# Batch 2's first dense layer by seven half-size products, with a new written order

## The chip, the cores and the metric

The kernel runs on one core of a Trainium2 chip. The metric is the device time of one execution in microseconds, the median of several runs. The engines are TensorE (PE; its weight loads are listed as PEld), VectorE (DVE), ScalarE (ACT), GpSimd (POOL) and SyncE (SP). PE multiplies into PSUM; DVE and ACT read PSUM; POOL does not touch it here. Every engine works through its own queue strictly in the order in which the instructions were written, and semaphores make it wait for the others. POOL and SP also issue the DMAs.

## The reference

Attention over four batches (8 heads, 768 positions, head size 64) in which a position sees the first 4 positions and the last 128, and then two dense layers with a squared ReLU between them:

```python
keep = (pos[None, :] < 4) | ((rel >= 0) & (rel < 128))
a = softmax(where(keep, q @ k.T / 8, -1e9))      # per batch and head
x = (a @ v), heads side by side                  # 3072 x 512
h = x @ w_in                                     # 512 x 2048
g = maximum(h, 0) ** 2
out = g @ w_out                                  # 2048 x 512, float32 out
```

## The kernel before

Products are in bf16 with float32 sums. The work goes batch by batch: loads, transposes of queries and keys (on PE for batches 0 and 1, by DMA transposes from SP for batches 2 and 3), scores, exps on ACT, masks on DVE or POOL, values, normalization on DVE, the transposed tokens `xT`, the first dense layer, ReLU and square, the second dense layer, evacuation, store. A batch has 768 tokens, handled as three slices of 256 (s = 0, 1, 2); attention's scores are made in pairs of head pairs for each slice.

**The first dense layer, plain** (`layer1`, L741). `w_in` lies in `w_in_sb` as 4 column groups by 4 row blocks. A group of output blocks is multiplied into one PSUM tile `pm` (L752), a ReLU goes from `pm` to `r` on ACT or DVE (L763, L765), and a square from `r` to `gT_sb` (L772, L774). For batches 1 and 2 there are eight groups of 512 tokens (slices 0 and 1) and four of 256 (slice 2).

**The first dense layer by seven products** (`layer1_fast`, L799, and `quad`, L845), in the kernel before for batch 3 alone. The token matrix, the weights and the output are each cut in two by two blocks. Seven products of sums and differences of blocks give the four output blocks for which eight would be needed otherwise (Winograd's or Strassen's scheme). The sums of weight blocks are `wi_sb[1, 2, 5, 6, 7]` (`weight_sums_in`, L781), made once on DVE; products 3 and 4 use `w_in_sb` itself. The sums of token blocks are made for slice 0 alone (halves of 128 columns, after a `spread` copy) and for slices 1 and 2 together (halves of 256 columns). Then `quad` runs twice for slice 0 and four times for slices 1 and 2. One `quad` works in the two PSUM banks of one tile `y`:

- product 1 into bank 0, product 2 into bank 1;
- `first` copies bank 0 to the SBUF tile `t`, and `less` subtracts bank 1 from `t`;
- product 5 overwrites bank 0, and `less` subtracts it from `t`;
- product 4 adds into bank 1, product 3 into bank 0;
- a ReLU of both banks goes to `r1`, and its square to `gT_sb`;
- product 6 adds into bank 0, product 7 into bank 1, `final` (a DVE instruction that adds `t` and clips at zero) goes to `r2`, and its square to `gT_sb`.

Each product there is 8 matmuls of 128 columns (slice 0) or 4 of 256.

**The second dense layer** (`layer2_fast`, L1006) is made by seven products in all batches but for the first two slices of batch 0. It needs four sums of blocks of `gT_sb` on DVE (L1029), and its results are put together on DVE and ACT (L1080 to L1143) in `osb`, which SP stores (L1148).

**Rooms.** PSUM has four tiles of two banks (`att` 2, `den` 2), which scores, values, transposes and both layers share. In SBUF the pool `qr` has five rooms: they hold loaded queries and keys (`qn`, two for a batch), one weight sum of the second layer for a while, and in the kernel before two of the five weight sums of the first layer; the other three lie in `qkT_all[0]`, where batch 2's transposed queries and keys were.

**The order.** Every piece of work is an `Op` in a plan. `ORDER` (L21 to L53) is a list of all ops by number, written out: the ops are emitted in that order, each on the engine that its letter names (d for DVE, a for ACT, g for POOL, otherwise its first choice), and so each engine's queue is fixed. Keys, planned durations, margins and groups in the code do not influence the program; they served the search that wrote the list. `after`, `takes` and `reads` bind the order and the rooms.

Of the kernel before, what the change touches and what calls it, by code (L numbers as in the profile page):

```python
# [13 lines left out]
BF16 = mybir.dt.bfloat16  # L14
# [6 lines left out]
ORDER = """  # L21
0 8 7 9 1 5 10 11 2 12 13 3 14 15 55d 57+0 16 19 59a 20 17 56d 21 18 61d 63+0 22 58 62d 65a 60d 64 6 67a 83+1 79 66a
68d 69+1 85 70 71d 103+0 84+0 105 73g 74d 72d 23 75+1 86 76 77d 91+0 78a 24 87+1 93 25 89 88 92+0 80 26 114+1 90 94
95+0 4 96 117 97 106g 99+1 98 104+0 107 100d 101 118g 81+1 102d 113+0 108d 156 115 127 82 116d 119+1 157a 121 27 28
120 109+0 111 29 30 31 32 33 158a 122 162 110 112 123+1 125 168 126a 124d 163d 171 169d 164d 165 172a 173d 159 166a
167a 128 131 130d 129d 177 160a 133a 132a 137 145 140 174 148 161d 178d 179d 136 144 289 290 146 149d 170d 147d 138
139d 134 141d 135 175d 34 208g 291 35 36 37 38 39 40 41 42 43 44 45 46 47 48 49 50 51 52 53 54 355 356 292 150 142
143 151 293 294 274 295 152 154 153d 296 297a 176a 298a 155d 186 275 187a 276 277 196+0 180 198a 183 181a 182a 184a
197 204+1 205 199d 188d 200+0 201 192+0 193 189 206a 207d 194d 203d 195d 190d 202a 219+0+0 191d 185d 357 358 359 220
222 278 279 212+0+1 213 215 300 209 301 280 281 373 385d 223 302 237+0+0 210+1 282 299 374 375 376 211 238 240 304  # L30
305 214 239d 306d 230+0+0 307 308 233 231 216 303 311 309d 310 217+0 221 224+0 312 315 234g 232g 313 218 360 314 225
235+0 283 316 241d 242+0 236 317a 284 243 361 362 363 364 365 366 367 368 369 370 371 226+1 228 251+0 229d 286a 227a
244+0 246 252d 253d 245a 285 247d 389 287d 248+1 390 392 340 249d 250d 256+0+0 341a 325 259 257 391 260d 393 326d
386 254+0 322 258g 382 255 342a 263+0+0 323a 261+1 334 262 324d 335d 264 266 265g 396 383 379 288 378 372 267d 331
397 399 398 327a 337 268+0 332d 377 380 384 381 269 319 338a 339d 270+0 271a 272 320d 400 273a 336a 333a 328 321d
329d 330d 456 394 401 352 343 437 353a 349 344a 402 395 530 560g 531 532 533 551 534 535 536 537 538 539 458 318 405
350a 457 351d 441 443d 439 438 345d 406 408 346 412 442 444 445 415 553 403 347d 413 447 409g 416g 428 348a 446a 549
554 548 407g 429 440 448 449 450 414d 451 460 387 354a 461 452 431 388 410 417 475 476 453 454a 479 411 432g 430g
480 463 481a 459 477 418 478 421 482 483 550 552 455 419 422 484a 424 555 404 465a 423g 425g 420 462a 485 433 486
487 490 464 434 488 426 672 489 466 427 467 468 471 580 540 541 542 543 544 545 491 492d 469 494 581 583 470 472  # L40
473d 503 670 495d 435 493 556 559 436 558 557 496a 564 500 565 567 504d 669 509 501d 566 587 510a 512 505a 588 590
568 561 673 511d 497 513d 571 515 574 671 498d 499a 569 572 506 502d 570 514d 516a 575 573 603 521 606 604 507d 522d
546 584g 591g 605g 547 527 576 562 577 518 517a 508a 528a 612 613 582d 631 632 633 519a 563 520a 589g 524 596 597
598g 578 474 579 529a 599 616 617 618a 614 525d 615 585 619 607g 635 592 620 623 586 523a 637a 674a 526d 621d 600d
636 601 625 593 594 622 675 608 638 609 641 602 634 678 624 627 610 626 628 629d 679+1 639 693+1 642 695d 650 651
681a 630 595 640a 680 682 683 694 697 611 654 643 646 656a 676 655 644 645 652 696 677 684 653 709 698 710 647 699
657 660 659a 658 661 708 700 648a 701d 685 686 707 662 665 703 702a 687a 663 664 666 688d 704 705 667a 689 739+0
741a 690 668 649 740 753+0 725+1 754 691 755a 711+1 757 743 706a 727a 726 712 742 756 758 744 692a 713a 745 746 729
714 759 715 760 747a 748a 749 750 767 728 730 716 761a 751 752d 731 732 733a 717 718 763 719a 735 736 764 721 722
769 762d 768 737 720a 738a 765 770 771 773a 772 774 775 778 723 766a 776a 734a 777 724d 779 782 780 786 787 790 791  # L50
792a 781 788 789 805 783 784a 793 794 797 795d 796 806 809 810 798 799 785 807 800 808 812 811d 815 801 802 803d 804
814d 813 816 818 819 824 817 820 821 822 823
"""  # L53
# [58 lines left out]
def kernel(  # L112
# [11 lines left out]
    nc = tc.nc  # L124
# [256 lines left out]
    def load_natural(b, s, older_values):  # L381

        begun = [ops["layer1", b - 2, 0, 0], w_out_op[3]]
        for ti in (1, 0):
            if s == 0:
                qn_slot[b, ti] = Slot("qr", NT)
            for i in range(2):
                t = 2 * s + i

                def run(e, t=t, ti=ti):  # L390
                    if t == 0:
                        qn_t[b, ti] = bank(qn_slot[b, ti], "qn", [128, NT, DM], BF16)
                    return [nc.gpsimd.dma_start(
                        out=qn_t[b, ti][:, t, :].rearrange("p (h d) -> p h d", d=D),
                        in_=(q, k)[ti][b, :, 128 * t:128 * t + 128, :].rearrange("h p d -> p h d"))]
                o = dma_op("pool", ("qk", b, ti, t), run, 64 * 0.032,
                           None,
                           [qn_slot[b, ti]] if t == 0 else ())
                o.after += begun
                o.margin = 1.661  # L400
        for t in (2 * s, 2 * s + 1):
# [13 lines left out]
    def attention(b, key):  # L415

        A = {}
        groups = GROUPS[b]
        begun = [ops["layer1", b - 1, 0, 0]] if b >= 2 else []
        prev_tr = [ops[x] for x in ops if x[0] == "transpose" and x[1] == b - 1]  # L420
# [356 lines left out]

    NAMES = (1, 2, 5, 6, 7)
    wi_sb, wi_slot = {}, {}

    def weight_sums_in(key, after):  # L781

        P.group = ("wi", 0)
        A = [[w_in_sb[:, 2 * i:2 * i + 2, 2 * j:2 * j + 2, :] for j in range(2)] for i in range(2)]
        spare = qkT_all[0].rearrange("p (n i a f) -> n p i a f", n=3, i=2, a=2)
        for n, (name, x, y, how) in enumerate(((1, A[0][0], A[1][1], ALU.add), (2, A[1][0], A[1][1], ALU.add),
                                               (5, A[0][0], A[0][1], ALU.add), (6, A[1][0], A[0][0], ALU.subtract),
                                               (7, A[0][1], A[1][1], ALU.subtract))):
            slot = Slot("qr", 99) if n >= 3 else None

            def run(e, n=n, name=name, x=x, y=y, how=how, slot=slot):
                if slot is None:
                    wi_sb[name] = spare[n]
                else:
                    wi_sb[name] = bank(slot, "wi", [128, 2, 2, 512], BF16)
                nc.vector.tensor_tensor(out=wi_sb[name], in0=x, in1=y, op=how)
            ops["wi", name] = op(key + 0.01 * n, {"dve": 1.26}, run, after=after, takes=[slot] if slot else [])

    def layer1_fast(b, ss, key, step):  # L799
# [23 lines left out]
        def total(names, x, y, how, n):  # L823
            pool = "qs" if len(names) == 1 else "expm"
            slot = Slot(pool, nq * len(names))
# [19 lines left out]
    def quad(b, ss, qd, key, xs, sums, slots, part, landed, whole):  # L845
# [8 lines left out]
        def weights(name, f, a):  # L854
            if name == 3:
                return w_in_sb[:, f // 4, a, f % 4:512:4]
            if name == 4:
                return w_in_sb[:, 2 + f // 4, 2 + a, f % 4:512:4]
            return wi_sb[name][:, f // 4, a, f % 4:512:4]

        def product(name, bk, n, fresh, after):
# [3 lines left out]
            def run(e):  # L865
# [4 lines left out]
                for i in range(nb):  # L870
                    for a in range(2):
# [3 lines left out]
                            skip_group_check=not (fresh and i == 0)), bk)  # L875
            need = [w_in_op[0], w_in_op[1], w_in_op[2], w_in_op[3]] if name in (3, 4) else [ops["wi", name]]
            o = op(key(n), {"pe": 0.45}, run, after=after + need + (landed if direct else [sums[name]]) + last[-1:],
# [23 lines left out]

        m1 = product(1, 0, 0, True, [])
        m2 = product(2, 1, 1, True, [])
# [263 lines left out]

    NATURAL, TURNED, BIASED, FAST = (2, 3), (), 1, (3,)
    load_sinks("act", 0)
# [23 lines left out]
    for b in range(B):  # L1193
# [9 lines left out]
        elif b in FAST:  # L1203
            weight_sums_in(b - 0.1, [ops[x] for x in ops if x[0] in ("scores", "sinks") and x[1] == 2])
            layer1_fast(b, (0,), lambda i, b=b: b + 0.167 * i / 2, 0.01)
# [4 lines left out]
        for i, fb in enumerate(range(0, NFB, 4) if b not in FAST else ()):  # L1210
            if b == 0:
                layer1(b, 0.2 + 0.226 * i / 4, range(fb, fb + 4), 512, 256, (2,))
            else:
                layer1(b, b + 0.34 + 0.167 * i / 4, range(fb, fb + 4), 512, 256, (2,))
        if b + 1 < B:
            if b + 1 in NATURAL:
# [52 lines left out]
```

## Time and profile before

| | us |
|---|---|
| median of 3 runs (212.92 to 213.13) | 212.99 |
| the profiled execution | 213.66 |
| its span, first to last instruction | 211.9 |
| PE busy | 204.0 |
| DVE busy | 167.8 |
| ACT busy | 112.9 |
| POOL busy | 97.9 |

The profile is of one execution. "Busy" is the time in which at least one instruction of the engine runs, so it is less than the sum of the instructions' durations where neighbours overlap. A group's row gives line, engine, operation, output and inputs, count, then busy time and mean nanoseconds of one, then the idle time of the engine just before these instructions and what ended it. The chain that ended last is followed back from the last instruction; its rows give start, microseconds and what was running. From 206.5 us on, DVE, ACT and the stores finish the last unit.

### The profile page before, as it was taken

How to read it: one execution, taken by the hardware profiler on the slowest of the kernel's cores; microseconds unless marked ns; L12 is line 12 of the kernel's file. 1: busy time of each engine (PE TensorE's matmuls, PEld its weight loads, DVE VectorE, ACT ScalarE, POOL GpSimd, SP SyncE). 2: the span in 40 equal slices, each digit the busy share in tenths (PEclk: the TensorE clock that was granted, in tenths of full speed). 3: DMA queues.
4: the chain of work that ended last, by engine and by line, in shares of the span. 5: the costliest groups of instructions: out<-in, count | busy, mean ns of one | idle time of the engine just before them, and what ended most of it. 6: DMA issues, size and time to landing. Idle time of an engine off the chain costs nothing.

```text
span 211.9 us, 5455 instructions
## 1 busy us (share of the span) xinstructions
PE 204.0 (96%) x2282; PEld 165.1 (78%) x2287; DVE 167.8 (79%) x303; ACT 112.9 (53%) x146; POOL 97.9 (46%) x139
## 2 busy tenths in 40 slices
PE   3999999999999999999999999999999999999993
PEld 3858997579569645589888964569899999998892
DVE  7487747795898847798776699997979989899963
ACT  2497277249652488567854234887931017976100
POOL 7989696598409965792851951216400000000000
PEclk9999999999999999999999999999999999999999
DMA  5999999999992999999933899304404504000205
GB/s 138 295 186 206 174 198 215 161 155 143 146 186 34 131 148 158 160 152 155 190 74 128 105 119 200 79 0 46 130 0 53 152 0 172 29 2 3 86 16 200
DMA packets 93625, 26.09 MB, mean 123 GB/s; under 512 B 86816, under 2 KB 91552, under 8 KB 93600
## 3 DMA queue, kind: packets, MB, share of 16 engines
q0 software_dynamic: 69248, 12.59, 83.1%
q1 hardware_dynamic: 24168, 13.07, 25.4%
q8 instruction: 18, 0.29, 0.6%
q10 hardware_dynamic: 184, 0.07, 0.1%
q14 instruction: 7, 0.06, 0.1%
HBM read 27.30 MB, written 6.29 MB: 159 GB/s over the span
## 4 chain that ended last, share of the span: by engine, by line
PE 95%; DVE 2%; POOL 1%; issue 1%; ACT 0%; DVEq 0%; POOLq 0%
PE pm L752 30%; PE py L1071 28%; PE pm L872 9%; PE po L671 7%; PE py L961 7%; PE ps L602 6%; PE pt L495 3%; PE pt L180 2%; PE px L720 1%; PE pk L561 1%; PE ps L595 1%; PE ya L1071 0%; DVE kblk L537 0%; DVE xn_sb L688 0%; POOL sg L213 0%
## 5 line engine op out<-in xcount | busy, mean ns | idle before, releaser
L752 PE MATMUL pm<-xT,w_in_sb 128*128 128x256 bf16 (+1 forms) x448 | 66.8, 304 | 0.0
L752 PEld LDWEIGHTS <-w_in_sb 128*128 128x128 bf16 x448 | 48.0, 114 | 12.6 <-issue 1.6
L623 ACT ACTIVATE expm<-ps 128x1024 bf16<-128x1024 f32 (+1 forms) x48 | 43.8, 952 | 17.7 <-PE ps L602 17.6
L213 POOL TENSOR_SCALAR_AFFINE_SELECT expm<-expm 128x512 bf16<-128x512 bf16 x38 | 26.6, 729 | 45.7 <-ACT expm L623 32.6
L1071 PEld LDWEIGHTS <-gT_sb 128*128 128x128 bf16 x336 | 31.0, 98 | 4.0 <-issue 0.7
L765 DVE TENSOR_SCALAR r<-pm 128x1024 bf16<-128x1024 f32 x19 | 23.2, 1221 | 3.3 <-PE pm L752 3.3
L1071 PEld LDWEIGHTS <-sg 128*128 128x128 bf16 x240 | 22.9, 98 | 3.2 <-issue 0.5
L763 ACT ACTIVATE r<-pm 128x1024 bf16<-128x1024 f32 x17 | 17.4, 1021 | 14.8 <-PE pm L752 14.8
L1071 PE MATMUL py<-wt,sg 128*128 128x256 bf16 x160 | 20.8, 273 | 0.0
L1071 PE MATMUL py<-wt,gT_sb 128*128 128x256 bf16 x160 | 20.6, 273 | 0.0
L772 ACT ACTIVATE gT_sb<-r 128x1024 bf16<-128x1024 bf16 x18 | 18.9, 1061 | 2.0 <-DVE r L765 1.9
L187 ACT ACTIVATE osb<-py 128x256 f32<-128x256 f32 (+1 forms) x15 | 6.4, 427 | 23.3 <-PE py L1071 7.9
L1071 PE MATMUL py<-w_out_sb,gT_sb 128*128 128x256 bf16 x144 | 18.7, 273 | 0.0
L688 DVE TENSOR_TENSOR xn_sb<-po,rc 128x512 bf16<-128x512 f32 (+1 forms) x28 | 17.2, 615 | 1.0
L671 PEld LDWEIGHTS <-expm 128*128 128x128 bf16 x352 | 16.3, 97 | 2.1 <-issue 0.5
L671 PE MATMUL po<-v,expm 128*128 128x65 bf16 x352 | 17.3, 193 | 0.1
L774 DVE TENSOR_TENSOR gT_sb<-r 128x1024 bf16<-128x1024 bf16 x18 | 13.6, 761 | 1.9 <-ACT r L763 1.8
L961 PE MATMUL py<-w_out_sb,gT_sb 128*128 128x512 bf16 x59 | 14.7, 380 | 0.4 <-issue 0.2
L602 PE MATMUL ps<-qkT 64*128 64x128 bf16 (+1 forms) x256 | 14.4, 238 | 0.0
L602 PEld LDWEIGHTS <-qkT 64*128 64x128 bf16 x256 | 8.1, 94 | 8.0 <-issue 6.3
L671 PE MATMUL po<-vs,es 128*128 128x65 bf16 x128 | 12.8, 193 | 0.0
L687 DVE RECIPROCAL rc<-po 128x8 f32<-128x8 f32 (+1 forms) x28 | 5.5, 196 | 8.4 <-PE po L671 8.3
(100 smaller groups left out, 336.5 us busy)
## 6 DMA issues: line engine op xcount, KB each, us to landing
out_dram<-osb SPq DMA_DIRECT2D x11, 512.0 KB, 3.3
v<-in_v_dram POOLq DMA_DIRECT2D x24, 128.0 KB, 6.9
qn<-in_k_dram POOLq DMA_DIRECT2D x20, 128.0 KB, 6.3
qn<-in_q_dram POOLq DMA_DIRECT2D x20, 128.0 KB, 6.4
w_in_sb<-in_moe_w_in_dram POOLq DMA_DIRECT2D x4, 512.0 KB, 9.3
w_out_sb<-in_moe_w_out_dram POOLq DMA_DIRECT2D x4, 512.0 KB, 9.2
qr<-in_k_dram SPq DMA_DIRECT2D x4, 256.0 KB, 5.3
qr<-in_q_dram SPq DMA_DIRECT2D x4, 256.0 KB, 5.0
```

The costliest lines, as they stand in the source:

```text
L213: nc.gpsimd.affine_select(out=e_tile, in_=e_tile, compare_op=ALU.is_ge, fill=fill, base=i - 1, pattern=[[0, n], [1 if i else -1, 128]], ch ...
L602: nc.tensor.matmul(ps[:, h2, o:o + w], lhsT=qkT_sb[r, m, 1, c, :], rhs=qkT_sb[r, m, 0, qb:qb + w // 128, :], start=(i == 0 and not biased) ...
L623: nc.scalar.activation(out=x[:, :, o:512], in_=bank_t["s", b, s, m][:, :, o:512], func=AF.Exp, scale=scale)
L671: touch(("po", b, s, m0), e, nc.tensor.matmul(pv[:, i, h2, :], lhsT=lhsT, rhs=rhs, start=(n_ == 0), stop=(n_ == len(mms) - 1)), j)
L688: touch(("po", b, s, m0), e, nc.vector.tensor_tensor(out=xn_sb[:, 2 * s:2 * s + 2, 128 * (m0 + j0):128 * (m0 + j0 + nj)].rearrange("p i (j ...
L752: nc.tensor.matmul(pm[:, i, :], lhsT=w_in_sb[:, fb // 4, kb, fb % 4:512:4], rhs=xT[:, c0 // 256:(c0 + cw) // 256, kb, :], start=(kb == 0), ...
L763: nc.scalar.activation(out=o, in_=h, func=AF.Relu)
L765: nc.vector.tensor_scalar_max(o, h, 0.0)
L772: nc.scalar.activation(out=g, in_=r, func=AF.Square)
L872: touch(tag, e, nc.tensor.matmul(y[:, bk, i, :], lhsT=weights(name, f0 + i, a), rhs=rhs[:, a, :], start=fresh and i == 0 and a == 0, stop= ...
L961: touch((b, u), e, nc.tensor.matmul(pm[:, i, :], lhsT=gT_sb[:, fb, 128 * t:128 * t + 128], rhs=w_out_sb[:, fb, :], start=(fb == 0), stop=( ...
L1071: ins = nc.tensor.matmul(y_, lhsT=x[:, i, :], rhs=r_, start=(first or tail and n == 2) and i == 0, stop=i == HB - 1, skip_group_check=not ...
```

## The change

Batch 2's first dense layer goes through `layer1_fast` too: `FAST` becomes `(2, 3)`. What comes with it:

- The weight sums are made before batch 2 rather than before batch 3, because batch 2 needs them too. They no longer lie in batch 2's `qkT_all[0]`. Sums 1, 6 and 7 go into two rooms of `qr`, which they keep; sums 2 and 5 are added in place into blocks of `w_in_sb`, after the sums that still read those blocks and after batch 1's first layer, which reads `w_in_sb` last. Each sum is made in two halves.
- Batch 3's loads of queries and keys come after the first of these sums.
- The fourth token sum of slice 0 (for products 6 and 7, 256 columns) takes a room of `qs` instead of one of `expm`.
- Batch 2's stores of its second and third unit use the row layout that the seven-product layer gives: two runs of 512 values for a partition instead of one of 1024.
- `ORDER` is new from end to end, with other choices of engine for many ops. Its first 200 numbers or so differ little.

```diff
-    NATURAL, TURNED, BIASED, FAST = (2, 3), (), 1, (3,)
+    NATURAL, TURNED, BIASED, FAST = (2, 3), (), 1, (2, 3)
...
-            weight_sums_in(b - 0.1, [ops[x] for x in ops if x[0] in ("scores", "sinks") and x[1] == 2])
...
+        if b + 1 == FAST[0]:
+            weight_sums_in(b + 0.4, [ops[x] for x in ops if x[0] == "layer1" and x[1] == b])
...
-    def weight_sums_in(key, after):
+    def weight_sums_in(key, last):
...
+        def room(e):
+            if not tiles:
+                tiles.extend(bank(s, "wi", [128, 3, 2, 512], BF16) for s in slots)
...
+        slots = [Slot("qr", 99), Slot("qr", 99)]
+        spec = ((1, A[0][0], A[1][1], ALU.add, (0, 0), (0, 1)), (6, A[1][0], A[0][0], ALU.subtract, (0, 2), (1, 0)),
+                (7, A[0][1], A[1][1], ALU.subtract, (1, 1), (1, 2)))
+        for n, (name, x, y, how, *places) in enumerate(spec):
+            for a, (d, j) in enumerate(places):
+                def run(e, name=name, x=x, y=y, how=how, a=a, d=d, j=j):
+                    room(e)
+                    wi_sb[name, a] = tiles[d][:, j]
+                    nc.vector.tensor_tensor(out=tiles[d][:, j], in0=x[:, :, a], in1=y[:, :, a], op=how)
...
+        for name, x, y, old in ((2, A[1][0], A[1][1], 6), (5, A[0][1], A[0][0], 7)):
+            for a in range(2):
+                def run(e, name=name, x=x, y=y, a=a):
+                    wi_sb[name, a] = x[:, :, a]
+                    nc.vector.tensor_tensor(out=x[:, :, a], in0=x[:, :, a], in1=y[:, :, a], op=ALU.add)
+                ops["wi", name, a] = op(key + 0.03 + 0.004 * a, {"dve": 0.7}, run, after=[ops["wi", old, a]] + last)
...
+                if b - 1 in FAST:
+                    o.after += [ops["wi", 1, 0]]
...
-            pool = "qs" if len(names) == 1 else "expm"
+            pool = "qs" if len(names) * hw <= 256 else "expm"
...
-            return wi_sb[name][:, f // 4, a, f % 4:512:4]
+            return wi_sb[name, a][:, f // 4, f % 4:512:4]
...
-        m1 = product(1, 0, 0, True, [])
+        m1 = product(1, 0, 0, True, [o for x, o in ops.items() if x[0] == "layer1" and x[1] == b - 1])
```

## The prediction

> **What bounds the kernel now.** I read the page's busy times and its 40 slices first, then the chain that ended last in order of time, then busy time by stage, then the groups of instructions with their shapes.
>
> ```profile
> span 211.9 us, 5455 instructions
> PE 204.0 (96%) x2282; PEld 165.1 (78%) x2287; DVE 167.8 (79%) x303; ACT 112.9 (53%) x146; POOL 97.9 (46%) x139
> ...
> PE   3999999999999999999999999999999999999993
> ...
> DVE  7487747795898847798776699997979989899963
> ```
>
> TensorE (PE) is full from the second slice to the last but one. Of the 7.9 us in which it is idle (211.9 - 204.0), all but 0.4 us lies before 17.4 us and after 206.5 us. So a microsecond of products taken away in the middle is a microsecond gained, unless something else then keeps PE waiting. VectorE (DVE) is the next fullest. By stage:
>
> ```profile
> core 0: us, PE busy (x) PEld busy (x) DVE busy (x) ACT busy (x) POOL busy (x), PEclk, DMA share, GB/s
> 74.00:98.00 24.00, 24.00 (x234) 15.96 (x232) 18.18 (x31) 16.61 (x20) 17.36 (x23) 1.00 1.73 154
> 98.00:124.00 26.00, 26.00 (x334) 22.28 (x333) 19.08 (x36) 13.02 (x18) 15.54 (x21) 1.00 0.91 128
> 124.00:150.00 26.00, 26.00 (x224) 16.92 (x223) 23.42 (x33) 18.61 (x21) 7.05 (x10) 1.00 1.04 98
> 150.00:176.00 26.00, 26.00 (x351) 24.15 (x352) 23.00 (x48) 9.03 (x15) 2.87 (x4) 1.00 0.25 50
> 176.00:190.00 14.00, 14.00 (x144) 13.95 (x142) 13.27 (x19) 10.99 (x14) 0.00 (x0) 1.00 0.20 77
> ```
>
> PE has no gap in any of these stages. Batch 2's first dense layer lies in 124 to 150 us, batch 3's, which already uses seven products, in 161 to 190 us. In the last row DVE is 95% busy (13.27 of 14.00) and PE still never waits. The granted clock is 1.00 throughout.
>
> **What the change removes on PE.** The chain prices both forms of the layer (columns: start, microseconds, what):
>
> ```profile
> 124.87 3.58 PE pm L752 x16
> 128.45 0.44 PE ps L602 x8
> 128.88 3.58 PE pm L752 x16
> ...
> 137.02 1.85 PE pm L752 x8
> 138.87 0.36 PE po L671 x12
> 139.24 1.73 PE pm L752 x8
> ...
> 145.83 3.62 PE pm L752 x32
> ...
> 161.74 0.45 PE pm L872 x8
> ...
> 164.38 1.79 PE pm L872 x32
> ...
> 175.81 14.04 PE pm L872 x144
> ```
>
> Batch 2 now: 64 products of 512 columns and 64 of 256. Eight of 512 take 1.73 us behind other full-array work, 1.85 behind scores; that 0.12 us belongs to the score groups, which stay. So 64 x 0.216 = 13.84. Sixteen of 256 take 1.75 (chain at 99.81 us), so 64 x 0.1094 = 7.00. Together **20.84 us**.
>
> Batch 2 after: the same code as batch 3, whose pieces are 112 products of 128 columns and 112 of 256 (the order confirms it: 224 of each where there were 112). Thirty-two of 128 take 1.79, or 55.9 ns each: 112 x 0.0559 = 6.26. The run of 144 is 32 small ones and all 112 large: (14.04 - 1.79) / 112 = 109.4 ns, so 12.25. Together **18.51 us**. PE saves **2.33 us**. If the 0.12 us behind each of six score groups went too, it would be 3.05; I do not count on it, since six score groups stay and each must stand before something.
>
> A page speaks against these prices. The Trainium skill, TensorE: Matmul & The Clock Gate, section "Back-to-back issue gap", says that in a real kernel each product is paired with a weight load and then costs about 81 ns at 128 columns and about 131 ns at 512. Estimated from that page the 112 small products would cost 9.07 us and the 64 large ones removed only 8.38, so the change would add work. This trace has 55.9 and 216 ns with a weight load before every product, and the sum goes by those.
>
> **What it adds on DVE and ScalarE (ACT).** From the groups by shape:
>
> ```profile
> L913 DVE TENSOR_TENSOR t<-t,pm 128x512 f32<-128x512 f32 x12 | 7.9, 683 | 0.7 <-ACT t L187 0.5
> L940 DVE CUSTOM_DVE_ANT_1 r<-pm,t 128x1024 bf16<-128x1024 f32 x6 | 7.1, 1217 | 0.0
> L187 ACT ACTIVATE t<-pm 128x512 f32<-128x512 f32 x5 | 3.0, 596 | 8.0 <-PE pm L872 8.0
> L896 DVE TENSOR_TENSOR gT_sb<-r 128x1024 bf16<-128x1024 bf16 x4 | 2.8, 688 | 0.0
> L796 DVE TENSOR_TENSOR wi<-w_in_sb 128x2048 bf16<-128x2048 bf16 x2 | 2.5, 1226 | 0.0
> ```
>
> In batch 2, on DVE: 12 subtractions x 0.683 = 8.2, 6 finals x 1.217 = 7.3, eight token sums (0.284 x 3 + 0.418 + 0.420 x 3 + 0.686 = 3.2), one bank copy 0.69, 4 squares x 0.69 = 2.8; gone are 8 ReLUs x 1.22 = 9.8 and 4 squares x 0.76 = 3.0. Net +9.4. Ten weight sums of half the size (nearest row, the same element count: 0.69) stand for five of 1.22: +0.8. On ACT: 5 bank copies x 0.596, a spread of 1.05, 6 ReLUs x 1.02 and 8 squares x 1.06 for 4 ReLUs and 8 squares: +6.1. The new order moves other work from DVE to ACT, so over the whole kernel DVE's rows grow by 5.1 us and ACT's by 11.4.
>
> None of this is on PE's path while DVE keeps up, so what counts is the stretch where it may not. I take it from the end of the products of the fifth group of batch 1's first layer to the end of batch 2's last product of the first layer, because the sums, the masks of batch 2 and the whole new layer lie there. In the order of the changed kernel PE has 62.9 us of work in it (three blocks of eight 512s, four of sixteen 256s, the 42 small products, 24 second-layer products of 0.873, scores, values and the rest by the chain's prices). DVE has 113 instructions there whose rows sum to 69.7 us: 20.8 for the new layer, 11.2 for 16 second-layer sums, 8.4 for 18 evacuations and their sums, 8.1 for nine normalizations, 7.9 for 13 masks, 7.0 for ReLUs and squares of batch 1, 5.5 for eight weight sums, 0.9 for small ones. Neighbouring DVE instructions overlap: in 150 to 176 us 48 rows sum to 27.0 and take 23.00 busy (0.083 each), in 98 to 124 us 36 sum to 21.7 and take 19.08 (0.073). With 0.08 the 69.7 become **60.7 us, 96% of the stretch**. The like stretch of the kernel before (58.6 us of PE) holds 53.8 us of rows, near 81%.
>
> **The wait that this makes.** The trace of before has no stage with this load for so long, so I bound it. Below: DVE is never idle, 60.7 fits in 62.9, PE waits 0. Above: DVE idles 10% as in 124 to 150 us (2.58 of 26) although there PE was the bound; 60.7 / 0.90 = 67.4, PE waits 4.5. I take 5% as in 176 to 190 us, the row nearest in kind (seven-product work): 60.7 / 0.95 = 63.9, which is 1.0; and with the late start of the first group (below) I say **1.1 us**.
>
> It shows first at the first group of seven. Product 2 reads weight sum 2, whose last half stands on DVE behind evacuations of batch 1's second layer. The group's first subtraction stands behind 3.3 us of such rows, and product 4 may not add into its bank before that subtraction has read it, with only 1.4 us of PE work after product 2.
>
> **Moved steps.** Weight sums 2 and 5 are added in place into `w_in_sb` and wait for batch 1's last first-layer product, 24 us of PE work ahead of their use; behind them on DVE stand second-layer sums and a normalization. POOL: batch 2's 18 loads (0.91 us each to issue) go out earlier; batch 3's first key load now waits for a weight-sum tile and for the transposes of batch 2, because two of five rooms hold weight sums, and masks stand behind it in the queue. Batch 3's last four tile loads go behind masks of its own second pair. From the first scores of that pair to the scores of the last pair PE has 24.7 us of work; the chain is 5.8 to the second scores, about 5.6 for exps, masks and two issues, 6.4 landing (page, qn), two to four transposes of 1.2 to 2.5 on SP: 20 to 23. Cost nothing, cover 2 to 4 us; beyond it PE, in order, loses each microsecond. The 12 sink values (1.7 us on POOL) trade places between batches. Batch 2's stores of units 1 and 2 write 2 KB runs for 4 KB; their tiles are wanted again only some 12 us later, landing is 3.3.
>
> **Sum.** -2.33 + 1.1 = -1.2. The profiled execution took 213.66 us, 211.9 span and 1.8 around it; it becomes 212.4 with a span of 210.7. It stands 0.67 above the median of the runs, 212.99, which becomes **211.8 us**.
>
> **Rivals.**
> - *Clean*: DVE keeps up as in 176 to 190 us; -2.33, or -2.6 with part of the 0.12s: 210.4 to 210.7. For: the same work ran there without a gap. Against: attention work was absent there.
> - *Swallowed*: waits of 1.9 to 2.7 us give 212.6 to 213.4, no measurable change. For: 96% load leaves 2.2 us of DVE room in 63.
> - *DVE becomes the bound* (other side): its idle time in the stretch is a tenth, waits 4.5, so +2.2: 215.2. It decides from the point where DVE idles over 4.3 us there (waits beyond 2.33), 7%. For: the mixed stages of before idle 10% and more. Against: there PE set the pace, so idle time was free.
> - *Batch 3 fed late*: keys or queries of its last tiles land 3 us past the cover; +0.7, 213.7 or above. Against: the cover above.
>
> **How the numbers follow.** Forecast (waits 0.3 to 1.9) 0.46, clean 0.14, swallowed 0.14, DVE bound 0.21, fed late 0.05. What a measurement here can tell from no change is about 0.2%, 0.43 us: faster is below 212.56, slower above 213.42. Forecast and clean are faster (0.60), swallowed is same, with little from the edges (0.14), the rest slower (0.26). Low is 210.4, clean's best; high is 214.4, within the DVE rival, which leaves about 0.12 above and 0.04 below. The forecast's own range is 211.0 to 212.6.
>
> **What would show it.** PE busy near 201.7 us; 224 first-layer products of 128 columns at 56 ns; no PE gap before the stretch; gaps put down to DVE's subtractions (L928 of the new file) or the weight sums at the first group of seven; DVE 90% or more busy through the stretch. I am wrong if PE's saving is not 2.3, if the waits are put down to ACT or transposes, or if they exceed 2.3.

## The result, and the profile after

The changed kernel takes 212.68 us (median of 20 runs, 211.95 to 213.39), the kernel before 213.16 in 20 runs beside them (212.36 to 214.61). The ratio of the means (212.60 to 213.27) is 0.9968, 95% interval 0.9954 to 0.9983: faster by 0.7 us, between 0.4 and 1.0. I had forecast 1.2 us, within a range that holds the result.

The page of the changed kernel, the lines that answer to those shown of before:

```profile
span 211.1 us, 5703 instructions
PE 202.7 (96%) x2379; PEld 169.7 (80%) x2383; DVE 171.3 (81%) x321; ACT 124.0 (59%) x160; POOL 98.0 (46%) x139
...
PE   3999999999999999999999999899999999999993
...
DVE  6487718569996766999897989999999869999863
```

PE now has an 8 in its row, in the slice that begins at 132 us. Busy time by stage around it:

```profile
core 0: us, PE busy (x) PEld busy (x) DVE busy (x) ACT busy (x) POOL busy (x), PEclk, DMA share, GB/s
111.00:123.20 12.20, 12.20 (x196) 10.66 (x194) 10.63 (x27) 3.48 (x5) 3.90 (x6) 1.00 0.78 111
123.20:130.00 6.80, 6.80 (x107) 6.12 (x106) 6.03 (x13) 5.84 (x8) 4.57 (x7) 1.00 0.66 120
130.00:136.00 6.00, 5.32 (x81) 4.64 (x79) 5.75 (x9) 5.25 (x7) 5.65 (x10) 1.00 0.63 42
136.00:143.00 7.00, 6.99 (x72) 6.69 (x71) 6.86 (x12) 6.45 (x8) 3.91 (x5) 1.00 1.49 100
```

The first group of seven (123 to 130 us) costs PE nothing. The idle time lies where slice 0's groups hand over to the groups of slices 1 and 2, and there DVE, ACT and POOL are all near full.

**The gaps.** PE's own rows there (start, duration, what, idle time before and who ended it):

```profile
131.64 0.51 PE L607 MATMUL ps<-qkT 64*128 64x256 bf16 x8
132.23 1.64 PE L887 MATMUL pm<-xs,wi 128*128 128x256 bf16 x20
133.71 0.53 PE L676 MATMUL po<-v,expm 128*128 128x65 bf16 x12
134.07 0.60 PE L887 MATMUL pm<-xT,w_in_sb 128*128 128x256 bf16 x4
134.95 0.60 PE L887 MATMUL pm<-xT,w_in_sb 128*128 128x256 bf16 x4 [0.28 <-ACT t L189]
135.87 0.60 PE L887 MATMUL pm<-xs,wi 128*128 128x256 bf16 x4 [0.31 <-DVE r L955]
```

From start to start four products of 256 columns need 4 x 0.109 = 0.44 us. Between 134.07 and 134.95 they took 0.88, between 134.95 and 135.87 0.92: **0.44** lost waiting for the third group's bank copy (`first`, L189 on ACT, 134.30 to 134.90, behind a square in ACT's queue), and **0.48** for the second group's `final` (L955), which frees the tile for the fourth group. The idle time in brackets is smaller, since the row's duration runs past the point at which the next product could start; so PE's "busy" includes part of such waits. In the same way 0.25 was lost before 132.23 (0.12 of it the usual change from scores; the rest waits for the first group's `final`), 0.15 within the 20 products for ReLU of the second group, and 0.17 before 140.36 for a token sum. Together **1.37 us**.

DVE over the same time:

```profile
130.95 1.23 DVE L955 CUSTOM_DVE_ANT_1 r<-pm,t 128x1024 bf16<-128x1024 f32 x1
132.09 0.55 DVE L637 TENSOR_TENSOR expm<-expm,mask 128x768 bf16<-128x768 bf16 x1
132.56 0.63 DVE L845 TENSOR_TENSOR xs<-xT 128x512 bf16<-128x512 bf16 x1
133.11 0.89 DVE L911 TENSOR_TENSOR gT_sb<-r 128x1024 bf16<-128x1024 bf16 x1
133.92 0.76 DVE L637 TENSOR_TENSOR expm<-expm,mask 128x768 bf16<-128x768 bf16 x1
134.60 1.21 DVE L955 CUSTOM_DVE_ANT_1 r<-pm,t 128x1024 bf16<-128x1024 f32 x1
135.74 0.67 DVE L928 TENSOR_TENSOR t<-t,pm 128x512 f32<-128x512 f32 x1
```

The second `final` stands behind a square and a mask and began at 134.60. It could have begun at about 133.98 (PE goes on to the values at 133.71; in pool_quiet and no_masks below it began 0.27 and 0.28 us after that point). And token sum, square and second mask took 0.63, 0.89 and 0.76 for their usual 0.42, 0.68 and 0.55: **0.63 us** more, all beside POOL's sink values:

```profile
131.79 2.47 POOL L548 TENSOR_TENSOR vs<-vs_in,head_rows 32x130 bf16<-32x130 f32 x4
```

The mask at 132.09 lay beside them too and kept its 0.55; the last section says what decides.

A second, smaller loss lies far ahead of the layer. The chain that ended last leaves PE there:

```profile
60.30 1.03 ACT expm L628
...
61.46 4.71 POOL expm L215 x6
66.17 0.85 POOL qn L396
67.03 1.24 POOL expm L215 x2
...
68.31 0.87 PE po L676 x23
```

Batch 1's last values wait for a POOL mask behind the issue of a batch 2 load (L396). From their first to the next product the 24 matmuls took 1.17 us (68.06 to 69.23), in the kernel before 0.94 (67.82 to 68.76): 0.2 us.

**The balance.** From the first product of batch 0's first layer to the last product group of the kernel PE took 189.31 us before (17.86 to 207.17) and 188.60 after (17.78 to 206.38), -0.71. The terms: -2.33 on products, +1.37 at the hand-over, +0.2 at 68 us; together -0.76.

### The profile page after: what moved, and what is told of

Read it like the earlier page. It is cut to its first block, busy times and chain, and to the rows that moved or that the text cites. A ratio compares the mean times of both kernels' runs of the same rounds, so it can differ in the third digit from the quotient of the medians.

```text
span 211.1 us, 5703 instructions
## 1 busy us (share of the span) xinstructions
PE 202.7 (96%) x2379; PEld 169.7 (80%) x2383; DVE 171.3 (81%) x321; ACT 124.0 (59%) x160; POOL 98.0 (46%) x139
## 4 chain that ended last, share of the span: by engine, by line
PE 89%; POOL 4%; DVE 3%; issue 1%; ACT 1%; POOLq 0%; DVEq 0%
PE py L1086 26%; PE pm L757 20%; PE pm L887 16%; PE py L976 7%; PE po L676 6%; PE ps L607 5%; PE pt L500 3%; POOL expm L215 3%; PE pt L182 2%; PE px L725 1%; DVE r L955 1%; PE ya L1086 1%; PE pk L566 1%; PE ps L600 1%; ACT expm L628 0%
## 5 line engine op out<-in xcount | busy, mean ns | idle before, releaser
L215 POOL TENSOR_SCALAR_AFFINE_SELECT expm<-expm 128x512 bf16<-128x512 bf16 x38 | 25.7, 707 | 43.5 <-ACT expm L628 39.2
L757 PE MATMUL pm<-xT,w_in_sb 128*128 128x256 bf16 (+1 forms) x320 | 44.7, 294 | 0.0
L757 PEld LDWEIGHTS <-w_in_sb 128*128 128x128 bf16 x320 | 34.2, 114 | 6.4 <-issue 0.8
L768 ACT ACTIVATE r<-pm 128x1024 bf16<-128x1024 f32 x15 | 15.4, 1025 | 12.9 <-PE pm L757 12.0
L887 PEld LDWEIGHTS <-w_in_sb 128*128 128x128 bf16 x256 | 21.7, 114 | 0.7 <-issue 0.6
L887 PE MATMUL pm<-xs,wi 128*128 128x128 bf16 (+1 forms) x192 | 19.5, 246 | 0.4 <-DVE r L955 0.3
L887 PEld LDWEIGHTS <-wi 128*128 128x128 bf16 x192 | 16.3, 114 | 1.7 <-issue 0.9
L928 DVE TENSOR_TENSOR t<-t,pm 128x512 f32<-128x512 f32 x24 | 16.0, 683 | 1.2 <-PE pm L887 0.6
L770 DVE TENSOR_SCALAR r<-pm 128x1024 bf16<-128x1024 f32 x9 | 11.0, 1222 | 7.1 <-PE pt L500 4.7
L189 ACT ACTIVATE osb<-py 128x256 f32<-128x256 f32 (+1 forms) x14 | 5.8, 413 | 17.6 <-DVE osb L1134 10.7
L955 DVE CUSTOM_DVE_ANT_1 r<-pm,t 128x1024 bf16<-128x1024 f32 x12 | 14.6, 1221 | 0.8 <-PE pm L887 0.5
## 6 DMA issues: line engine op xcount, KB each, us to landing
w_out_sb<-in_moe_w_out_dram POOLq DMA_DIRECT2D x4, 512.0 KB, 11.1
```

Of the source, the lines that this page charges most:

```text
L215: nc.gpsimd.affine_select(out=e_tile, in_=e_tile, compare_op=ALU.is_ge, fill=fill, base=i - 1, pattern=[[0, n], [1 if i else -1, 128]], ch ...
L757: nc.tensor.matmul(pm[:, i, :], lhsT=w_in_sb[:, fb // 4, kb, fb % 4:512:4], rhs=xT[:, c0 // 256:(c0 + cw) // 256, kb, :], start=(kb == 0), ...
L768: nc.scalar.activation(out=o, in_=h, func=AF.Relu)
L887: touch(tag, e, nc.tensor.matmul(y[:, bk, i, :], lhsT=weights(name, f0 + i, a), rhs=rhs[:, a, :], start=fresh and i == 0 and a == 0, stop= ...
L928: touch(tag, e, nc.vector.tensor_tensor(out=T["t"], in0=T["t"], in1=T["y"][:, bk], op=ALU.subtract), bk)
L955: touch(tag, e, nc.vector._custom_dve(TENSOR_ADD_SAT, out=r.rearrange("p b n c -> p b (n c)"), in0=T["y"].rearrange("p b n c -> p b (n c)" ...
```

## The experiments

PE's order is the same in all of these kernels, so the distances between its landmarks compare them far more sharply than whole times, which also carry a start that differed by up to 1.0 us between executions. This table has the change against the changed kernel's profile, one execution of each (the columns run from landmark to landmark, at the changed kernel's times: the first product of the first layer, two products of batch 1's first layer, scores ahead of the hand-over, a second-layer product behind it, the last group), and the ratio to the kernel before; the changed kernel's ratio is 0.9968 [0.9954, 0.9983].

| | 17.8-90.9 | 90.9-97.2 | 97.2-126.4 | 126.4-144.8 | 144.8-206.4 | ratio [95%] |
|---|---|---|---|---|---|---|
| mask_behind | +0.12 | 0 | 0 | **+0.44** | +0.04 | 1.0012 [0.9993, 1.0030] |
| both | -0.23 | +4.63 | 0 | **+0.43** | 0 | 1.0016 [0.9997, 1.0034] |
| no_masks | 0 | 0 | 0 | **-0.71** | +0.18 | 0.9978 [0.9955, 1.0000] |
| double_masks | +0.15 | +0.32 | 0 | **+3.58** | 0 | 1.0153 [1.0108, 1.0198] |
| sinks_early | +0.15 | +0.11 | 0 | **+0.46** | 0 | 0.9996 [0.9984, 1.0007] |
| act_first | +0.10 | 0 | 0 | **0** | 0 | 0.9960 [0.9944, 0.9975] |
| sinks_act | +0.11 | 0 | 0 | **+0.47** | 0 | 1.0006 [0.9989, 1.0022] |
| double_sums | +0.18 | +1.43 | +0.42 | **0** | 0 | 1.0048 [1.0028, 1.0069] |
| pool_quiet | -0.22 | +0.35 | 0 | **-0.50** | +0.34 | 0.9979 [0.9963, 0.9995] |
| quiet_act | +0.14 | +1.30 | 0 | **-0.50** | +0.52 | 0.9983 [0.9967, 1.0000] |
| quiet_masks | +0.10 | +0.90 | 0 | **+0.06** | 0 | 0.9979 [0.9961, 0.9997] |
| fed | +0.11 | +1.13 | 0 | **+0.34** | 0 | 1.0000 [0.9984, 1.0017] |

The edits are in `ORDER` unless shown otherwise. Its numbers here: 521 `final` of the second group, 518 its square, 571 `first` of the third group, 572 and 574 its subtractions; 642 and 640 masks of batch 3's first slice on DVE; 627 sink values of batch 3, 656 its third pair of POOL mask halves, 610 to 614 its loads.

### mask_behind: the mask ahead of `final`

```diff
-518a 642 636 521 571a 570
+518a 636 521 642 571a 570
```

> In the changed kernel PE loses about 1.5 us between 131.9 and 140.4 us, in five places; the largest, 0.48 us before 135.87, is product 1 of the fourth group, which waits for `final` of the second group (L955, 134.60 to 135.81) to free its PSUM tile. That `final` could have started at 133.75 but stood in DVE's queue behind a mask of batch 3 (L637, 133.92 to 134.68). Here this mask goes behind that `final`. Theory 'order in the queue': `final` ends 0.6 us earlier, the gap before the fourth group's product 1 goes from 0.48 to nearly 0, nothing else gets later, and the kernel gains 0.4 to 0.5 us on the changed one (about 212.2). Theory 'DVE is full': DVE is busy without a break from 130.95 to 142 us, so an order cannot give it time; the wait comes back within some 5 us at another DVE instruction (the subtractions L928 or the token sum L845), and the time stays within 0.2 us of the changed kernel.

The gap closed, as the first theory said, and came back larger one and a half microseconds later. PE in mask_behind:

```profile
134.78 0.60 PE L887 MATMUL pm<-xs,wi 128*128 128x256 bf16 x4
135.21 0.60 PE L887 MATMUL pm<-xT,w_in_sb 128*128 128x256 bf16 x4
136.24 0.60 PE L887 MATMUL pm<-xs,w_in_sb 128*128 128x256 bf16 x4 [0.43 <-DVE t L928]
```

1.03 us from 135.21 to 136.24, so 0.60 lost behind a subtraction that the mask now delays, and 0.20 and 0.12 more after it, for the 0.48 that closed: 0.44 slower in all. The order had nothing to give there. "DVE is full" is right on the place, and even it did not foresee a loss.

### both: mask and bank copy

```diff
-    sizes = dict(att=2, den=2, qr=5, qs=6, expm=8, r=3, osb=2, sg=4, u=2)
+    sizes = dict(att=2, den=2, qr=5, qs=6, expm=9, r=3, osb=2, sg=4, u=2)
-569+0 641 519 520 518a 642 636 521 571a 570
+569+0 641 571a 519 520 518a 636 521 642 570
```

> As in mask_behind, and the bank copy of the third group (`first`, L189 on ACT, 134.30 to 134.90, for which PE waits 0.44 us before 134.95) goes ahead of the square of the second group on ACT. That needs a ninth room in the pool `expm`, since the copy's tile t lay in a room that a values product reads until 134.1. Theory 'order in the queue': both gaps (0.44 and 0.48) go but for 0.2 to 0.3 that `final` still needs, so 0.6 to 0.7 us faster than the changed kernel, about 212.0. Theory 'DVE is full': as mask_behind, within 0.2 us of the changed kernel, the gaps reappearing behind DVE before 142 us.

The 0.44 behind ACT went; the 0.48 before the fourth group stayed, and 0.60, 0.20 and 0.12 came behind the subtractions: +0.43. No gain. (The 4.63 at 94 us is another matter, in the account of the prediction.)

### no_masks and double_masks: the dose

```diff
-                            if s == 0:
+                            if s == 0 and b == 3:
+                                return
+                            if s == 0:
```

> Leaves out the four masks of batch 3's first slice (L637 on DVE; 0.55, 0.55, 0.76 and 0.55 us at 128.19, 132.09, 133.92 and 136.33), so batch 3's attention for the first 256 positions is not masked. Nothing else changes. Theory 'DVE is full': 2.4 us of rows leave the stretch of 128 to 137 us, more than the 1.5 us that PE loses, so nearly all five gaps close: 1.2 to 1.5 us faster than the changed kernel, about 211.3. Theory 'order in the queue': only the two masks ahead of the second `final` count, 1.0 us of rows, so that `final` starts when its products end (133.75) and 0.5 to 0.6 us are gained, about 212.1; the 0.44 us for ACT's bank copy stays. Theory 'the ring of PSUM tiles' (PE has too little other work between a group's last product and the next tile): the gaps stay within 0.3 us.

-0.71: the gaps of 0.48 and 0.17 went, the 0.25, 0.15 and 0.44 stayed to 0.01. So both theories are half right. Of the 1.37 us about half is DVE's load. The other 0.7 (0.13 + 0.15 + 0.44) is the way from PE to a reader of its banks and back, with too little other PE work in between; less work on DVE does not shorten it. The 0.44 also holds ACT's order, since `first` stands behind a square there: act_first below takes that gap away. The 0.25 and the 0.15 stood in all of these kernels, to 0.02. Further on 0.18 was given back at 149 us.

```diff
                                 nc.vector.tensor_mul(x[:, :, 128:512], x[:, :, 128:512], mk)
+                                if b == 3:
+                                    nc.vector.tensor_mul(x[:, :, 128:512], x[:, :, 128:512], mk)
```

> The same four masks are done twice (a 0/1 mask, the same values), so DVE has 2.2 to 2.4 us more in the stretch. Theory 'DVE is full': each microsecond is lost by PE, 2.0 to 2.4 us slower than the changed kernel, about 214.9. Theory 'order in the queue': only those ahead of the second `final` and of the first subtraction count, 1.0 to 1.3 us slower, about 213.8. If there were room on DVE: within 0.3 us.

+3.58 for four instructions of 0.56, more than "DVE is full" allowed. PE in double_masks:

```profile
136.36 0.60 PE L889 MATMUL pm<-xT,w_in_sb 128*128 128x256 bf16 x4 [0.28 <-ACT t L189]
138.95 0.60 PE L889 MATMUL pm<-xs,wi 128*128 128x256 bf16 x4 [1.99 <-DVE r L957]
```

2.59 us from start to start: the gap before the fourth group alone grew to 2.15. Two things were added beyond the time of the masks: a repeated mask reads what the first one wrote and started 0.59 us after it (128.28, 128.87), where neighbours otherwise follow after 0.47, and beside POOL's masks two token sums took 0.95 and 0.85 for 0.42, square and mask 1.12 and 0.98 for 0.68 and 0.55.

### sinks_early: POOL beside DVE

```diff
-435g 433g 442g 504a
+435g 433g 442g 627g 504a
...
-649g 658g 627g 610
+649g 658g 610
```

> In the changed kernel three 16-bit DVE instructions in the full stretch took 0.21 us each more than the same forms elsewhere (token sum 0.627 at 132.56 for 0.415, square 0.889 at 133.12 for 0.683, mask 0.755 at 133.93 for 0.546), and each of them lay beside POOL's sink values of batch 3 (L548, four TENSOR_TENSOR, 131.79 to 134.26). Here these four POOL instructions go 15 us earlier in POOL's queue, behind its last mask of batch 2, where POOL was idle from 116.9 to 125.4. DVE's and PE's instructions keep their order. Theory 'POOL slows DVE': the three take 0.42, 0.68 and 0.55 us, DVE gains 0.6 us in the full stretch, and since DVE is what PE waits for there, the gap of 0.48 before the fourth group and the 0.17 at 140.2 close: 0.5 to 0.6 us faster than the changed kernel, about 212.1. Rival 'it was not POOL': the three stay as long, and the time stays within 0.2 us of 212.7.

Slower by 0.46, and yet the mechanism showed itself. DVE and POOL in sinks_early:

```profile
132.38 0.85 DVE L845 TENSOR_TENSOR xs<-xT 128x512 bf16<-128x512 bf16 x1
133.15 1.11 DVE L911 TENSOR_TENSOR gT_sb<-r 128x1024 bf16<-128x1024 bf16 x1
134.19 0.55 DVE L637 TENSOR_TENSOR expm<-expm,mask 128x768 bf16<-128x768 bf16 x1
```

```profile
131.33 0.90 POOL L396 DMA_DIRECT2D qn<-in_k_dram  x1
132.23 1.49 POOL L215 TENSOR_SCALAR_AFFINE_SELECT expm<-expm 128x512 bf16<-128x512 bf16 x2
133.68 1.78 POOL L396 DMA_DIRECT2D qn<-in_q_dram  x2
```

POOL's masks moved up into the room that the sink values had left, and beside them the same DVE instructions lost 0.43 us each instead of 0.21: when each began, its POOL mask had 0.57 us to go, the sink values 0.34. The mask at 134.19, beside no POOL computation, took its 0.55. The second `final` came later, not earlier, and the gap before the fourth group grew from 0.48 to 0.93.

### act_first and sinks_act: ACT's part

```diff
-569+0 641 519 520 518a 642 636 521 571a 570
+569+0 641 571a 519 520 518a 642 636 521 570
```

(with the ninth room of `expm`; sinks_act has the edit of sinks_early too)

> Only the ACT part of both: `first` of the third group (L189) ahead of the second group's square on ACT, with a ninth room in `expm`; masks as in the changed kernel. Theory 'ACT causes its gap': 0.44 us faster than the changed kernel, about 212.2. Theory 'DVE is full': the gap of 0.44 before product 5 goes, but the fourth group's product 1 still waits for the `final` that DVE ends at 135.8, so its gap grows from 0.48 to 0.9 and the time stays within 0.2 us of 212.7.

The stretch took the same 18.37 us to 0.01: the gap of 0.44 went, the one before the fourth group grew from 0.48 to 0.92. The copy on ACT is not what sets the time.

> sinks_early and act_first together. If POOL slows DVE and DVE is what holds PE, the two add up where each alone is limited: `final` of the second group ends 0.6 us earlier and product 5 of the third group no longer waits, so of the 1.5 us that PE loses 0.9 to 1.0 comes back: 211.7 to 211.8. If the waits just move to the next DVE instruction, no better than sinks_early.

+0.47, as sinks_early: one gap of 1.39 us, from the same `final`.

### double_sums: load further ahead

```diff
                     nc.vector.tensor_tensor(out=tiles[d][:, j], in0=x[:, :, a], in1=y[:, :, a], op=how)
+                    nc.vector.tensor_tensor(out=tiles[d][:, j], in0=x[:, :, a], in1=y[:, :, a], op=how)
```

> The six halves of weight sums 1, 6 and 7 (L803, 0.68 us each, between 77 and 97 us) are made twice, so DVE has about 3.7 us more (six times 0.68 less the overlap of neighbours), all of it before the first group of seven. Theory 'one full stretch' (the prediction's model: 60.7 us of DVE in 62.9 of PE, so any work there counts once the 2.2 us of room are gone): 1.5 to 3 us slower than the changed kernel, 214.2 to 215.7. Theory 'only the last 10 us are full' (DVE is 88 to 95% busy before 123 us, with PE never waiting, and idle for 1.01 us at 113.4 and 0.67 at 124.9): DVE makes it up before the first group of seven; 0 to 0.5 us slower.

In size (+2.0 between the landmarks) the first theory, in place neither. At the hand-over nothing changed, to 0.01 us: what DVE is given before 100 us does not reach the layer. But PE lost 1.85 us on the spot. Its waits between 85 and 112 us in double_sums:

```profile
PE ps L607 <- DVE xn_sb L693: 0.8, 1, 0.8
PE po L676 <- DVE expm L637: 0.3, 1, 0.3
PE py L1087 <- DVE sg L1045: 0.2, 1, 0.2
```

In the changed kernel DVE is busy for 6.16 of the 6.20 us from 91.0 to 97.2 and PE just does not wait. So there are two full stretches with a pause between them, not one, and the first is full to the brim without costing anything.

### pool_quiet, quiet_act, quiet_masks: POOL silent during the hand-over

pool_quiet: the edit of sinks_early, and

```diff
-                                    triangles(y[:, i], i, 4)
+                                    ins = triangles(y[:, i], i, 4)
+                                    if (b, s, m, i) == (3, 1, 2, 0):
+                                        after_dma(ins, held[0])
...
+            if (b, f0, len(ss)) == (2, 0, 1):
+                held.append(ins)
...
-642 636 521 571a 570
+642 636 521 656g 611 612 613 614 571a 570
```

> In sinks_early POOL's masks (L215) moved into the place that the sink values had left, and slowed the same DVE instructions by more (token sum 0.85 us, square 1.11, against 0.42 and 0.68 alone), so PE's gap before the fourth group grew from 0.48 to 0.93 us. Here the sink values are early too, and POOL's third pair of mask halves, with the loads behind it, waits for the `final` of the second group, as late as it ran in the changed kernel; so POOL computes nothing from about 131.5 us to the end of that `final`. Theory 'POOL slows DVE, and DVE holds PE': the square takes 0.68 us, the mask before the `final` 0.55, `final` ends 0.5 to 0.6 us earlier than in the changed kernel, the gap before the fourth group closes; 0.4 to 0.5 us faster than the changed kernel by the stretch from 18 us to the last product, a ratio to the kernel before of about 0.9945. Rival 'the slowdown has another cause' (place in the order, weight loads): square and mask stay at 0.89 and 0.76, ratio 0.997.

DVE in pool_quiet:

```profile
132.49 0.42 DVE L847 TENSOR_TENSOR xs<-xT 128x512 bf16<-128x512 bf16 x1
132.83 0.68 DVE L913 TENSOR_TENSOR gT_sb<-r 128x1024 bf16<-128x1024 bf16 x1
133.43 0.56 DVE L637 TENSOR_TENSOR expm<-expm,mask 128x768 bf16<-128x768 bf16 x1
133.91 1.22 DVE L957 CUSTOM_DVE_ANT_1 r<-pm,t 128x1024 bf16<-128x1024 f32 x1
```

All as expected: the three are back at 0.42, 0.68 and 0.56, `final` follows at 133.91, the gap before the fourth group is gone, and the stretch is 0.50 us shorter. That POOL's work beside these three cost PE 0.5 us is shown. But the kernel did not get faster (0.9979), for two reasons that the table places: 0.34 was given back at 149 us, where the score products now waited for queries and keys of batch 3, and 0.35 was lost at 94 us. PE at 149 us:

```profile
149.00 0.62 PE L607 MATMUL ps<-qkT 64*128 64x128 bf16 x12 [0.28 <-DMA qkT<-qn]
```

> pool_quiet with `first` of the third group ahead of the second group's square on ACT (and a ninth room of `expm`). Alone, act_first turned its gap of 0.44 into 0.44 more at the fourth group, since `final` came at the same time. With `final` 0.6 us earlier some of it should now count: gap before product 5 gone, gap before the fourth group 0.2 to 0.35; 0.55 to 0.75 us faster than the changed kernel, ratio about 0.9935. If `final` is not earlier, as act_first: ratio 0.996 to 0.997.

The hand-over as forecast (0.30 before the fourth group, nothing before product 5), but no better than pool_quiet: -0.50 again, since of the 0.44 that product 5 gains the wait for `final` takes 0.30 at once. 0.52 was given back at 149 us.

quiet_masks is quiet_act with this:

```diff
-642 636 521
+636 521
...
-585a 640 574 637
+585a 574 642 640 637
```

> quiet_act, and the two masks of batch 3's second pair of head pairs (L637) behind the `final` of the second group and both subtractions of the third group on DVE, since only a values product 4 us later needs them. In mask_behind one of them delayed those subtractions, which cost more than it gave. Theory 'each DVE instruction in line counts by when its result is wanted': `final` ends some 0.25 us earlier than in quiet_act and no subtraction later, so the gap before the fourth group closes: 0.7 to 1.0 us faster than the changed kernel, ratio about 0.992. If DVE is simply full, the wait comes back behind the subtractions or the masks before 142 us: as quiet_act.

`final` was not earlier: it started at 134.32, 0.28 us after PE had gone on to the values (134.04), after DVE had stood idle for 0.41. The profile puts that down to ACT's `first`, which ended at 134.29; its own products end no sooner either. So the 0.32 before the fourth group is a round trip, not DVE's load. And the masks behind the subtractions pushed back a normalization (L695), for which the values at 138.77 waited 0.55. Once more an order that relieves one instruction charges the next.

### fed: batch 3's loads first

```diff
-649g 658g 627g 610 656g 611 612 613 614
+649g 658g 610 611 612 613 614 656g
```

(with 627 behind 442, and the edit of act_first)

> From pool_quiet and quiet_act: with `final` of the second group 0.6 us earlier the gap before the fourth group closed or fell to 0.30, but the score products at 149 us then waited 0.44 and 0.62 us for the transposed queries and keys of batch 3's last tiles (SP's L454), which they had not done in the changed kernel. Here the sink values are early, `first` of the third group stands ahead of the square on ACT, and POOL's third pair of mask halves goes behind the four loads that stood behind it, instead of waiting for `final`: these loads are issued 2.5 to 4 us earlier than in the changed kernel, and the masks start where the loads end, near 136 us, when `final` is over. Theory 'batch 3's feeding has no cover': no wait at the scores near 149 us, the gaps of 131 to 141 us as in quiet_act (0.25, 0.15, 0.30, 0.17), and from 96 us to the last product 0.55 to 0.7 us less than in the changed kernel. Rival 'the scores at 149 us wait for something else': the wait there stays at 0.4 to 0.6. A wait at batch 2's scores near 94 us, 0 to 1.1 us so far from one execution to the next, is not touched, so the ratio to the kernel before lies between 0.9935 and 0.998.

The wait at 149 us was gone, with SP's transposes starting at 138.22 for 141.6 before: so it was the loads of batch 3 that the scores there had waited for. But the hand-over got 0.34 slower. DVE and POOL in fed:

```profile
133.31 1.12 DVE L911 TENSOR_TENSOR gT_sb<-r 128x1024 bf16<-128x1024 bf16 x1
134.35 0.98 DVE L637 TENSOR_TENSOR expm<-expm,mask 128x768 bf16<-128x768 bf16 x1
```

```profile
133.04 1.77 POOL L396 DMA_DIRECT2D qn<-in_q_dram  x2
...
136.52 1.60 POOL L215 TENSOR_SCALAR_AFFINE_SELECT expm<-expm 128x512 bf16<-128x512 bf16 x2
```

The two lost 0.43 each, the loss that POOL's masks cause, while the profile shows only the issue of loads there and the masks three microseconds later. In the 14 profiles of this case 379 of 387 such DVE instructions beside issues alone ran at their usual speed, to 0.06 us, and six more lost 0.10 to 0.12. A square and a mask in double_masks have the same 1.12 and 0.98, with POOL's masks beside them. So the masks probably ran earlier in fed than their rows say (their wait was recorded as met at 132.91, and spans on POOL are rough); that is not settled.

No kernel tried is faster than the changed one by more than its interval; act_first (0.9960) is the same.

## Why the prediction was right or wrong

- **PE's saving, 2.33 us: right.** 224 products of 128 columns stand in the profile after (96 + 64 + 64 in the groups by shape), and the prices held. The chain after:

```profile
161.82 1.79 PE pm L887 x32
...
175.91 12.27 PE pm L887 x120
```

  Thirty-two small ones in 1.79 again, 55.9 ns; 16 small and 104 large are 0.89 + 11.38 = 12.27. The Trainium skill (TensorE: Matmul & The Clock Gate, "Back-to-back issue gap") has 81 ns for the small ones in such a stream; these rows decide against it. PE busy fell by 1.3 only, to 202.7 for my 201.7, since it includes parts of waits.
- **DVE's rows and share: right.** From 85.5 to 150.84 us DVE was busy for 61.3 us; I had 60.7, and 5% idle where it was 6%; the 61.3 hold the 0.63 that POOL cost. PE's work in the stretch was 64.0 (65.3 less the 1.37), where I had added up 62.9. ACT grew by 11.1, forecast 11.4.
- **"The wait that this makes", 1.1 us: near in size (1.37), wrong in place and model, so the size was luck.** I had one stretch of 63 us with an average load, and the first wait at the first group of seven. There PE lost nothing. double_sums shows that the load of the first half does not arrive at the second, and no_masks that half of the wait is not DVE's load but the round trip of a bank through ACT or DVE, ACT's order included. What counted was the local order in 10 us in which three groups were in flight.
- **"Moved steps ... cost nothing": the step that failed.** The sink values, which I let "trade places between batches" for nothing, stretched three DVE instructions by 0.63 us; with POOL silent there (pool_quiet) PE got 0.50 back, which is part of the 1.37. A batch 2 load ahead of batch 1's last masks cost 0.2 at 68 us. These 0.2 and the 0.27 by which the wait exceeded 1.1 are the difference between my -1.2 and the -0.7.
- **The cover for batch 3's tiles, "2 to 4 us": wrong.** In the changed kernel the last transpose landed at 148.86, 0.36 us ahead of the scores at 149.22. In no_masks PE came 0.71 us earlier to these scores and waited 0.18; in pool_quiet, with the loads 0.4 later, it waited more. The rival "batch 3 fed late" did not decide, but it caps what the hand-over can give back.
- **A cover that I did not look at.** The first scores of batch 2's second slice stand at 94.45 in the changed kernel, 3.4 us after the eighth of SP's row of transposes ended (91.06). The semaphore of the transpose that they need was complete at 93.97, half a microsecond ahead; in the kernel before at 91.29 for scores at 98.21. In seven of the twelve experiments' profiles they waited for it, 0.1 to 1.3 us and in `both` 3.0, though the order ahead of them was the same. PE in quiet_act (two rows) and in `both` (the third):

```profile
93.83 0.23 PE L607 MATMUL ps<-qkT 64*128 64x128 bf16 x2
95.00 0.56 PE L607 MATMUL ps<-qkT 64*128 64x256 bf16 x10 [0.94 <-DMA qkT<-qn]
...
97.23 0.56 PE L607 MATMUL ps<-qkT 64*128 64x256 bf16 x10 [2.80 <-DMA qkT<-qn]
```

  In `both` the granted clock then stood at 0.50 for 3.41 us from 97.94 on, which cost PE the other 1.7 of its 4.63. The changed kernel's own profile has no such wait; whether some of its runs have is not known, since only one execution of each kernel is traced.
- **The rivals.** "Clean" and "DVE becomes the bound" did not come; the result lies just above the forecast's own range (211.0 to 212.6), at the lower end of "swallowed"; the kernel before was 213.16 in these runs, 0.17 above the 212.99 that I started from. The threshold of the rival "DVE becomes the bound" was added up wrongly: 2.2 of room and 2.33 are 4.5 us of idle time, not 4.3. Nothing was put down to transposes in the profile after, and to ACT only the 0.44 that act_first showed to be worth nothing.

## What to carry to other kernels

When PE is full and a change takes work from it, look for the 10 us in which several PSUM tiles are handed over at once, and replay each reader of a bank there with its queue; an average load over a long stretch gave the right size here but not the place, and no remedy. Moving one instruction out of the way in a full queue only helps if the next one has slack, which none had in the orders tried here. Count what other engines do at the same moment, and the cover of every transfer on the way: gains at one place were given back at the next one, as soon as its cover of half a microsecond was used up.

## What the runs showed of the hardware

- A 16-bit DVE TENSOR_TENSOR with both operands in SBUF that begins while POOL computes loses what is left of the POOL instruction, less 0.14 us. In the 14 profiles 125 began with more than 0.15 us of a POOL TENSOR_TENSOR or AFFINE_SELECT to go, and all of them lost that, to 0.02 us: 0.21 with 0.34 to go (0.42 to 0.63, 0.68 to 0.89, 0.55 to 0.76), 0.43 with 0.57 to go (0.42 to 0.85, 0.68 to 1.11). Of 56 that began with less to go all but one kept their time, as the mask at 132.09 with 0.09 to go, and so did 79 of 81 beside which POOL's instruction began later. There POOL's instruction can be the longer one: the four sink values took 0.39, 0.66, 0.49 and 0.76 in the changed kernel, and 0.39 to 0.40 each in double_masks, beside a DVE instruction that reads PSUM.
- DVE instructions that read PSUM kept their time beside the same POOL work (L928 0.67 at 135.74, L955 1.23 at 130.95). The Trainium skill (SBUF — State Buffer, "Who interferes with whom") has this pair of conditions: two SBUF inputs contend with a POOL instruction that reads SBUF, one does not. It also says ("SBUF: two separate sides") that whichever starts first holds the shared ports for its whole instruction and the other is blocked; these rows agree, but for the 0.14 us.
- The time from the end of SP's eighth transpose to scores that waited for it differs between executions of one order: in quiet_act the scores resumed 1.26 us after it ended, in `both` 3.66.
